# First k and q ahead of the weights, table work reordered, fourteen weight tiles in flight with borrowed buffers spread over them

## Chip, cores, metric

One core of a Trainium2 chip. The metric is device time in microseconds (us) of one execution. Ratios are computed from the mean time of one kernel's runs over the mean of the other's runs of the same rounds, so they are not quite the ratio of the medians that stand beside them.

## The reference, cut to what matters

A linear ("hedgehog") attention over 8 batches, 8 heads, 576 tokens and head size 64 is followed by a spectral mixing layer on the 512 channels:

```python
k_p, q_p = phi(k), phi(q)              # exp of +- (x @ w_phi - max|x @ w_phi|)
kv = einsum('bhsf,bhsd->bhfd', k_p, v);  z = k_p.sum(2)
x = (q_p @ kv) / (q_p . z + 1e-6)      # -> (8, 576, 512)
X = rfft(x, axis=1)[:, :64]            # 64 modes
Yr = Xr @ w_r - Xi @ w_i               # w_r, w_i: 64 x 512 x 512 float32, one matrix per mode
Yi = Xr @ w_i + Xi @ w_r
u = x + irfft(Y, n=576);  out = u + relu(u @ w_ch)
```

The two weight tensors are 67 MB each. They are what most of the run consists of loading.

## The kernel before

Channels are worked in four groups `g` of 128 (two heads each). A group's attention has four units (two batches each), 16 units in all, numbered `n` in a software pipeline. When the four units of group 0 are done, its 16 weight tiles (8 modes of `w_r` or `w_i`, 128 x 8 x 512, cast by the load from float32 to bf16, 1 MB) can be mixed in. Long before that, weights are loaded ahead, into a pool of eight buffers and into "borrowed homes": tensors that are not used yet.

```python
def home(g, w):                      # where weight tile w of group g lives
    if g == 0 and w < 2:             # yacc: two homes
        t = yacc...[:, 4096 * w:4096 * w + 4096]
    elif g == 0 and w == 2:          # the other group's XT buffer
        t = XTb[1]...
    elif g == 0 and w in (10, 11):   # xs of groups 2 and 3
        t = xs[:, w - 8]...
    else:
        return pw.tile([128, MG, DMODEL], BF16, name="wt", tag="wt")   # pool, bufs=8

def next_w(n):                       # issue the next n weight loads, on POOL's DMA queue
    for _ in range(n):
        if wq: key = wq.pop(0); wts[key] = wload(*key)

def some(n):                         # do the next n mixes
        key = mixq.pop(0); mix(*key, wts.pop(key), ...)
        if key == (0, 2): clear(XTb[1])
        if key not in held: next_w(1)        # a freed pool buffer takes the next tile
held = [(0, mg) for mg in (0, 1, 2, 10, 11)] # borrowed homes: nothing handed back
# --- start (cut) ---
units[0].load_k(); next_w(1)         # k0, weight 0, then the identity, then q0, v0
...
units[1].load_k(); units[1].load_v(); next_w(1); units[1].load_q()
for n in range(-2, 17):              # the pipeline over units (cut)
    ...   # group 0's mixes begin at n == 4: some(2), some(1), some(1), some(4)
    if R:  R.turn_k(..); unit(n + 4).load_k()   # k of a later unit into the buffer just turned
           R.turn_q(..); unit(n + 4).load_q()
    if n < 3: next_w((1, 3, 3, 2, 2)[n + 2])    # 2 + 11 = 13 tiles before the first mix
```

Loads of k, q and weights go through one queue, POOL's, in the order of issue; v goes through SP's queue. The traces show an engine keeping to the order of its program: in the kernel before, PE's first row products need only kT, which ACT had copied by 12.2 us, but they stand behind the transposes of q0 and start at 17.29.

## Time and profile before

| kernel before | |
|---|---|
| median (3 runs ahead of the prediction; 4 with the result) | 466.84; 466.88 us |
| span of the profiled run | 467.1 us |
| q0 landed; first row products on PE | 16.02; 17.29 us |
| landing to landing in a full queue: weight tile; k or q tile | 5.05; 1.42 us |
| first weight load that waited for a freed pool buffer, issued | 107.2 us |
| last weight landed; from there to the end | 422.89; 44.2 us |

The landings are read from the trace, DMA by DMA. First the page of the kernel before: the span in 40 slices of 11.7 us, with the DMA engines' busy share in tenths and what they moved.

```profile
DMA  8999999999999999999999999999999999992797
GB/s 193 207 177 220 226 210 228 229 229 136 225 208 229 229 213 222 229 209 227 229 229 207 229 207 208 207 207 207 207 214 214 216 216 211 207 177 50 241 317 254
```

The digit is 9 almost everywhere, so the kernel looks evenly bound by DMA until slice 36. The second row shows what the first hides: the third slice moved 177 and the tenth 136 GB/s, where weights alone run at 207 and v loads lift a slice to 229. The same in windows of 4 us (busy time of each engine with its number of instructions, granted PE clock, DMA share, GB/s):

```profile
core 0: us, PE busy (x) PEld busy (x) DVE busy (x) ACT busy (x) POOL busy (x), PEclk, DMA share, GB/s
28.00:32.00 4.00, 3.35 (x26) 2.58 (x25) 0.69 (x2) 3.22 (x6) 2.01 (x3) 1.00 1.03 159
32.00:36.00 4.00, 2.99 (x23) 1.76 (x24) 3.44 (x5) 3.88 (x6) 2.05 (x3) 1.00 1.07 152
...
104.00:108.00 4.00, 1.75 (x19) 1.16 (x19) 2.59 (x7) 3.20 (x10) 0.78 (x1) 0.93 0.70 117
108.00:112.00 4.00, 4.00 (x54) 3.35 (x52) 1.07 (x4) 1.47 (x4) 0.58 (x2) 0.64 0.92 137
112.00:116.00 4.00, 4.00 (x63) 3.14 (x63) 1.83 (x4) 3.01 (x6) 3.14 (x5) 1.00 1.18 169
```

The share adds up the packets' times, so it passes 1 where packets overlap, and a full queue shows 1.2 and over here; these are the two stretches where it ran dry. The timeline of POOL, which issues, tells why for the second (start, length, what, and in brackets how long POOL sat idle and for whom):

```profile
90.51 0.70 POOL L37 DMA_DIRECT2D kb<-in_k_dram  x1 [12.26 <-PE one L37]
91.63 0.71 POOL L37 DMA_DIRECT2D qb<-in_q_dram  x1 [0.42 <-PE one L37]
107.22 0.89 POOL L37 DMA_DIRECT2D wt<-in_moe_w_i_dram  x1 [14.87 <-PE one L37]
111.53 0.70 POOL L37 DMA_DIRECT2D kb<-in_k_dram  x1 [3.42 <-PE one L37]
```

POOL had nothing it was allowed to issue for nearly 15 us: all homes were full, and the q tile issued at 91.63 was the last in the queue; it landed at 108.23. Last, the start on PE, and PE's last two mixes of a weight tile:

```profile
16.07 1.28 PE L37 MATMUL one<-ident_b,qb 128*128 128x128 bf16 x10 [8.98 <-DMA qb<-in_q_dram]
17.29 1.89 PE L37 MATMUL two<-w2blk,kT 128*128 128x256 bf16 x8
...
417.88 0.67 PE L37 MATMUL pt<-wt,XT 128*32 128x512 bf16 x8 [0.73 <-DMA wt<-in_moe_w_r_dram]
422.94 0.67 PE L37 MATMUL pt<-wt,XT 128*32 128x512 bf16 x8 [1.67 <-DMA wt<-in_moe_w_i_dram]
```

PE waits 8.98 us for q0, and at the end it waits for the last weight tile. After that come 44 us that can't begin earlier.

### The profile page before, as it was taken

To read this page: it belongs to the slowest core of one execution; us is meant where nothing else is said; L and a number is where in the kernel's file an instruction comes from. 1 tells how busy PE (TensorE), PEld (TensorE's weight loads), DVE (VectorE), ACT (ScalarE), POOL (GpSimd) and SP (SyncE) were. 2 spreads that over 40 slices of the span, in tenths; PEclk is the share of its full clock that TensorE was granted. 3 is DMA by queue.
4 is the path that set the end of the run, shared out by engine and by line. 5 is a ranking of instruction groups with operands and counts; after the bars stand their busy time and mean duration, and the time that the engine had idled before them with its cause. 6 is when DMAs were issued, how large, how long until landed. Compare 5 with 4: busy or idle time off the path is not lost.

```text
span 467.1 us, 9757 instructions
## 1 busy us (share of the span) xinstructions
PE 337.8 (72%) x4084; PEld 207.5 (44%) x4084; DVE 269.1 (58%) x488; ACT 281.1 (60%) x475; POOL 92.7 (20%) x130
## 2 busy tenths in 40 slices
PE   0377677758788777788768778129997656997991
PEld 0246465636565555466546546005443322332330
DVE  5275877564666566777675676563331113773882
ACT  2566988766787786688777765123443323664771
POOL 5130322104112121122210112203221110000331
PEclk9998999888888798799997989659998997999996
DMA  8999999999999999999999999999999999992797
GB/s 193 207 177 220 226 210 228 229 229 136 225 208 229 229 213 222 229 209 227 229 229 207 229 207 208 207 207 207 207 214 214 216 216 211 207 177 50 241 317 254
DMA packets 86301, 99.27 MB, mean 213 GB/s; under 512 B 2800, under 2 KB 79728, under 8 KB 86256
## 3 DMA queue, kind: packets, MB, share of 16 engines
q0 software_dynamic: 77264, 81.80, 102.9%
q1 hardware_dynamic: 8992, 16.85, 11.8%
q8 instruction: 32, 0.52, 0.4%
q14 instruction: 13, 0.11, 0.1%
HBM read 163.64 MB, written 9.44 MB: 371 GB/s over the span
## 4 chain that ended last, share of the span: by engine, by line
issue 37%; DMA 21%; PE 16%; ACT 8%; POOL 8%; DVE 7%; POOLq 0%; ACTq 0%
PE pt L37 8%; DMA wt<-in_moe_w_r_dram 8%; DMA wt<-in_moe_w_i_dram 6%; DMA kb<-in_k_dram 5%; PE one L37 4%; POOL wt L37 4%; PE two L37 4%; DVE m L37 4%; ACT AQ L37 3%; DMA qb<-in_q_dram 3%; POOL out_dram L37 2%; ACT AB L37 2%; DVE zall L37 2%; ACT qT L37 1%; ACT kT L37 1%
## 5 line engine op out<-in xcount | busy, mean ns | idle before, releaser
L37 ACT CAST xw<-pt 128x512 bf16<-128x512 f32 x72 | 42.0, 586 | 59.5 <-PE pt L37 58.3
L37 ACT ACTIVATE AB<-two 128x1024 bf16<-128x1024 f32 x64 | 62.8, 1051 | 7.5 <-DVE mk L37 5.1
L37 ACT ACTIVATE AQ<-two 128x1024 bf16<-128x1024 f32 x64 | 63.1, 1055 | 2.8 <-PE two L37 2.6
L37 PE MATMUL pt<-wchb,xT 128*128 128x512 bf16 x144 | 38.6, 393 | 19.3 <-DVE xT L37 19.3
L37 DVE TENSOR_REDUCE m<-two 128x8 f32<-128x1024 f32 x32 | 39.2, 1224 | 19.4 <-PE two L37 19.3
L37 DVE TENSOR_REDUCE mk<-two 128x8 f32<-128x1024 f32 x32 | 38.9, 1219 | 19.5 <-PE two L37 19.0
L37 POOL DMA_DIRECT2D wt<-in_moe_w_i_dram x30 | 26.5, 882 | 110.1 <-PE one L37 63.8
L37 POOL DMA_DIRECT2D wt<-in_moe_w_r_dram x29 | 25.6, 881 | 95.7 <-PE one L37 62.0
L37 DVE TENSOR_TENSOR va<-vn,ee 128x1152 bf16<-128x1152 f32 x32 | 42.0, 1356 | 0.0
L37 DVE RECIPROCAL rd<-one 128x6 f32<-128x6 f32 x48 | 9.4, 196 | 50.3 <-PE one L37 50.3
L37 ACT COPY kT<-one 128x512 bf16<-128x512 bf16 (+1 forms) x32 | 19.2, 640 | 30.0 <-PE one L37 30.0
L37 PEld LDWEIGHTS <-minus 96*128 96x128 bf16 x288 | 27.4, 114 | 20.1 <-issue 14.8
L37 DVE TENSOR_TENSOR xs<-pt,xs 128x512 bf16<-128x512 f32 x36 | 24.3, 691 | 18.9 <-PE pt L37 18.5
L37 PE MATMUL two<-qT,w2blk 128*128 128x512 bf16 x64 | 29.9, 467 | 6.3 <-ACT AQ L37 6.3
L37 PEld LDWEIGHTS <-XT 128*32 128x32 bf16 x512 | 18.0, 179 | 35.9 <-issue 22.9
L37 PE MATMUL two<-w2blk,qT 128*128 128x256 bf16 x128 | 21.2, 292 | 16.5 <-ACT AB L37 11.9
L37 DVE COPY xT<-pt 128x512 bf16<-128x512 bf16 x36 | 15.1, 422 | 27.9 <-PE pt L37 27.9
L37 PEld LDWEIGHTS <-xs 128*128 128x128 bf16 x304 | 24.1, 98 | 14.9 <-issue 7.6
L37 PE MATMUL two<-mT,minus 96*128 96x128 bf16 x256 | 30.3, 252 | 0.0
L37 PE MATMUL pt<-wt,XT 128*32 128x512 bf16 x208 | 18.6, 434 | 13.6 <-DMA wt<-in_moe_w_i_dram 9.9
L37 PEld LDWEIGHTS <-qT 128*128 128x128 bf16 x144 | 14.4, 103 | 31.3 <-issue 28.4
L37 DVE TENSOR_TENSOR xs<-one,rd 128x384 bf16<-128x384 f32 x48 | 26.8, 558 | 1.6
(113 smaller groups left out, 679.3 us busy)
## 6 DMA issues: line engine op xcount, KB each, us to landing
wt<-in_moe_w_i_dram POOLq DMA_DIRECT2D x30, 1024.0 KB, 23.7
wt<-in_moe_w_r_dram POOLq DMA_DIRECT2D x29, 1024.0 KB, 23.9
vn<-in_v_dram SPq DMA_DIRECT2D x16, 576.0 KB, 7.8
kb<-in_k_dram POOLq DMA_DIRECT2D x16, 288.0 KB, 17.6
qb<-in_q_dram POOLq DMA_DIRECT2D x16, 288.0 KB, 17.7
out_dram<-of SPq DMA_DIRECT2D x16, 256.0 KB, 5.8
out_dram<-of POOLq DMA_DIRECT2D x16, 256.0 KB, 5.3
yacc<-in_moe_w_r_dram POOLq DMA_DIRECT2D x1, 1024.0 KB, 12.5
```

What stands on the lines that cost most here:

```text
L37: ins = f(*args, **kwargs)
```

## The change

Its intent: let the first unit begin at once, and never let the weight queue run dry. (1) k0 and q0 lead the queue; weight 0 follows after the iotas and the identity. On DVE the memsets and the sine table come first, the identity and the small copies after it. (2) The second weight tile is one that goes to XT (tile 5) and it is issued after q1; two tiles, not one, follow q2. (3) Fourteen tiles before the first mix, and the six borrowed homes are spread over the tiles (0, 3, 5, 9, 12, 13), so that already the second mix hands back a pool buffer.

```diff
-        if g == 0 and w < 2:
-            t = yacc...[:, 4096 * w:4096 * w + 4096]
-        elif g == 0 and w == 2:
+        if g == 0 and w in (0, 9):
+            h = w // 9
+            t = yacc...[:, 4096 * h:4096 * h + 4096]
+        elif g == 0 and w == 5:
             t = XTb[1]...
-        elif g == 0 and w in (10, 11):
-            t = xs[:, w - 8]...
+        elif g == 0 and w in (3, 12, 13):
+            t = xs[:, max(w - 10, 1)]...
     order = list(wq)
+    wq.remove((0, 5))
+    wq.insert(1, (0, 5))
     units[0].load_k()
-    next_w(1)
-    ident_f = ...; make_identity(nc, ident_f)
-    ident_b, minus, m3s: copies and memsets on DVE
     units[0].load_q()
     units[0].load_v()
     (iotas)
-    w2blk: memset and copies on DVE
+    ident_f = ...; make_identity(nc, ident_f)
+    next_w(1)
+    memsets of w2blk, m3s, CF, XT on DVE
     (sine table on DVE and ACT)
+    ident_b, w2blk, minus: copies on DVE
-                if key == (0, 2):
+                if key == (0, 5):
                     clear(XTb[1])
-    held = [(0, mg) for mg in (0, 1, 2, 10, 11)]
+    held = [(0, mg) for mg in (0, 3, 5, 9, 12, 13)]
     units[1].load_k()
     units[1].load_v()
+    units[1].load_q()
     next_w(1)
-    units[1].load_q()
-            next_w((1, 3, 3, 2, 2)[n + 2])
+            next_w((2, 3, 2, 3, 2)[n + 2])
```

(The views are shortened to "...", and moved lines are told in words.)

More of the change, by code (lines that the diff above doesn't have):

```diff
@@ L316, in home @@
     def home(g, w):
-        if g == 0 and w < 2:
-            t = yacc.bitcast(BF16).rearrange("p o e -> p (o e)")[:, 4096 * w:4096 * w + 4096]
-        elif g == 0 and w == 2:
+        if g == 0 and w in (0, 9):
+            h = w // 9
+            t = yacc.bitcast(BF16).rearrange("p o e -> p (o e)")[:, 4096 * h:4096 * h + 4096]
+        elif g == 0 and w == 5:
             t = XTb[1].rearrange("p s b m -> p (s b m)")[:, 0:4096]
-        elif g == 0 and w in (10, 11):
-            t = xs[:, w - 8].rearrange("p b n d -> p (b n d)")[:, 0:4096]
+        elif g == 0 and w in (3, 12, 13):
+            t = xs[:, max(w - 10, 1)].rearrange("p b n d -> p (b n d)")[:, 0:4096]
         else:
@@ L355 @@
     units[0].load_k()
-    next_w(1)
-    ident_f = scr[:, 2176:2304]
-    make_identity(nc, ident_f)
-    ident_b = const.tile([128, 128], BF16, name="ident_b")
-    dve.tensor_copy(ident_b, ident_f)
-    for t in range(3):
-        r = slice(32 * t, 32 * t + 32)
-        dve.tensor_scalar_mul(out=minus[r], in0=ident_f[r, r], scalar1=-1.0)
-    for m3 in m3s:
-        dve.memset(m3, 0.0)
     units[0].load_q()
@@ L373 @@
     pool.iota(mi, [[4, 2], [8, NO], [1, 4]], base=0, channel_multiplier=0)
-    w2blk = const.tile([128, 256], BF16, name="w2blk")
-    dve.memset(w2blk, 0.0)
-    dve.tensor_copy(w2blk[0:64, 0:128], wpf[0:64, :])
-    dve.tensor_copy(w2blk[64:128, 128:256], wpf[64:128, :])
+    ident_f = scr[:, 2176:2304]
+    make_identity(nc, ident_f)
+    next_w(1)
     def clear(x):
@@ L382, in clear @@
             dve.memset(x[:, i:i + 2], 0.0)
-    clear(XTb[0])
+    w2blk = const.tile([128, 256], BF16, name="w2blk")
     wchb = const.tile([128, 4, 512], BF16, name="wchb")
     CF = const.tile([128, 6, 4, 64], BF16, name="CF")
+    ident_b = const.tile([128, 128], BF16, name="ident_b")
     sf = const.tile([128, 5], F32, name="sf")
+    mf = scr[:, 2112:2176]
+    dve.memset(w2blk, 0.0)
+    for m3 in m3s:
+        dve.memset(m3, 0.0)
+    dve.memset(CF[:, 4:6], 0.0)
+    clear(XTb[0])
     dve.tensor_copy(sf, si)
-    mf = scr[:, 2112:2176]
     dve.tensor_copy(mf, mi)
@@ L410 @@
     act.activation(csf, ang, ACT.Sin, scale=2.0 * math.pi / S_)
+    dve.tensor_copy(ident_b, ident_f)
+    dve.tensor_copy(w2blk[0:64, 0:128], wpf[0:64, :])
+    dve.tensor_copy(w2blk[64:128, 128:256], wpf[64:128, :])
+    for t in range(3):
+        r = slice(32 * t, 32 * t + 32)
+        dve.tensor_scalar_mul(out=minus[r], in0=ident_f[r, r], scalar1=-1.0)
     def forward_table():
-        dve.memset(CF[:, 4:6], 0.0)
         for p0, p1, d, n in ((0, 128, 0, 4), (0, 64, 4, 1), (64, 128, 5, 1)):
```

## The prediction

> What bounds it. The weight stream. In the page's slices the DMA share is 9 nearly everywhere to slice 36. Between landings (issue and landing times of each DMA) a weight tile of 1 MB (bf16) takes 5.05 us, a k or q tile 1.42, and a v load lengthens the gap it falls into by about 1.65. That is 207 GB/s written as bf16, about 414 GB/s read as float32; the Trainium skill, "DMA: Bandwidth & Descriptors", section Bandwidth, measures 425 GB/s for large loads by one core, so the stream has no spare rate. The last weight lands at 422.9 us and its matmuls start at 422.94 after waiting for it; what follows (to 467.1) is a fixed tail of 44 us. So time is won only where the DMA queue runs dry before 422.9.
>
> Where it runs dry (windows of 2 and 3 us, GB/s):
> - 30 to 38 us: 113, 162, 141, 192. The fourth k tile waits until 29.6 us for unit 1's transposes. From landings, about 3.0 us lost.
> - 105 to 120 us: 89, 120, 202, 136, 194. All 13 homes are full; the first mixes (96.4 us) use borrowed homes, which hand no pool buffer back, so the next weight is issued only at 107.2 us. About 4.4 us lost.
> - 0 to 4 us: start, not touched.
>
> What the change does.
> 1. q0 goes ahead of weight 0. Before, q0 landed at 16.02 and PE idled from 7 to 16.07 us. Now q0 should land at 8 to 9. The DVE chain for the sine table now precedes the bf16 identity, so k0's transposes move from 5.9 to about 7 us, which does not matter. The first row products move from 17.3 to about 9.8 us: the attention stage is about 7.4 us earlier throughout, as PE, ACT and DVE pace it (13 to 18 us a unit), and each unit's k and q still land before use.
> 2. Another weight goes ahead of k2, and two follow q2. At about 22 us, when k3 is issued, the queue holds work to about 37 us. The dry stretch at 30 us goes: -3.0 us.
> 3. A fourteenth tile: 5.05 us more work before the first mix. The queue then lasts to about 110 us, and the second mix frees a pool buffer at about 90. The dry stretch at 105 us goes: -4.4 us.
> 4. Moved memsets and copies (2 to 3 us of DVE, 0.3 of POOL): off the path.
>
> On the critical path: items 2 and 3, 7.4 us less a few tenths, as long as compute is as early as the stream, which item 1 gives. I expect 6.6 us: 466.84 -> 460.2 us (-1.4%). Range 458 to 463.5. Chances: faster by over 2% 0.08; within 2% 0.91; slower 0.01.
>
> What would show it: q0 landed before 9 us; first row products near 10; no window between 10 and 400 us under 200 GB/s; last weight landed near 416; last mix still waiting for it; tail near 44 us.
>
> What would make it wrong: PE, not DMA, ending last in the final stage (PE is busy all the time from 394 to 417 us, and waits for the last two tiles only 0.73 and 1.67 us), so that a faster stream is worth less; a later dry stretch because attention did not keep its 7 us; k or q tiles late behind the deeper queue. A gain over 2% would need the tail or the stream's rate to change, which nothing here does.

## The result

| | before | after |
|---|---|---|
| median with the result (4 runs each) | 466.88 us | 461.85 us (460.21 to 462.25) |
| ratio, 95% interval | | 0.9885 (0.9852 to 0.9917) |
| median in a later set of rounds, on chip 6 (11 and 6 runs) | 467.57 us | 461.11 us (460.41 to 461.92) |
| ratio, 95% interval | | 0.9870 (0.9828 to 0.9912) |
| span profiled | 467.1 us | 460.2 us |
| q0 landed; first row products | 16.02; 17.29 us | 10.38; 11.64 us |
| first freed pool buffer reloaded | 107.2 us | 94.6 us |
| last weight landed; from there to the end | 422.89; 44.2 us | 416.38; 43.8 us |

A gain of 1.2 to 1.3%, within 2%. The profiled run of the kernel before took 468.84 us, 2.0 us over its median, and that of after 461.99, about its median; so the profiles show a larger gain (6.9 us in the span) than the first medians (5.0), and about that of the later ones (6.5). The lines of after that answer to those shown of before; first the slices of the page:

```profile
DMA  8999999999999999999999999999999999992897
GB/s 192 207 216 220 230 229 209 228 229 207 229 230 209 228 229 227 209 230 229 207 229 228 207 207 207 206 208 207 207 213 218 214 211 211 205 178 55 249 323 252
```

The digits are nearly the same; in the second row the 177 and the 136 are gone. The windows:

```profile
28.00:32.00 4.00, 3.78 (x79) 3.05 (x79) 3.01 (x3) 3.49 (x5) 0.45 (x1) 1.00 1.24 207
32.00:36.00 4.00, 2.48 (x28) 1.68 (x22) 2.62 (x4) 3.37 (x8) 0.00 (x0) 1.00 1.16 264
...
104.00:108.00 4.00, 4.00 (x43) 3.41 (x42) 1.10 (x3) 1.82 (x4) 0.70 (x1) 0.50 1.23 207
108.00:112.00 4.00, 4.00 (x61) 3.15 (x61) 2.81 (x6) 2.49 (x4) 2.94 (x4) 0.92 1.23 207
112.00:116.00 4.00, 2.88 (x48) 1.84 (x47) 3.43 (x5) 4.00 (x6) 1.14 (x2) 1.00 1.25 207
```

The timeline of POOL around the first freed buffers:

```profile
86.55 0.70 POOL L37 DMA_DIRECT2D kb<-in_k_dram  x1 [10.43 <-PE one L37]
88.31 0.71 POOL L37 DMA_DIRECT2D qb<-in_q_dram  x1 [1.07 <-PE one L37]
94.61 0.87 POOL L37 DMA_DIRECT2D wt<-in_moe_w_r_dram  x1 [5.59 <-PE one L37]
96.21 0.87 POOL L37 DMA_DIRECT2D wt<-in_moe_w_i_dram  x1 [0.73 <-PE one L37]
```

The q tile issued at 88.31 lands only at 110.71, so at 94.61 the queue still held 16 us of work. The start and the end on PE:

```profile
10.42 1.28 PE L37 MATMUL one<-ident_b,qb 128*128 128x128 bf16 x10 [1.62 <-DMA qb<-in_q_dram]
11.64 1.89 PE L37 MATMUL two<-w2blk,kT 128*128 128x256 bf16 x8
...
411.36 0.68 PE L37 MATMUL pt<-wt,XT 128*32 128x512 bf16 x8
416.42 0.67 PE L37 MATMUL pt<-wt,XT 128*32 128x512 bf16 x8 [1.67 <-DMA wt<-in_moe_w_i_dram]
```

The attention stage starts 5.65 us earlier, and the last weight lands 6.5 us earlier and is still waited for. The 44 us behind it did not change.

### The profile page after: what moved, and what is told of

It is laid out like the page before. It is cut to its first block, busy times and chain, and to the rows that moved or that the text cites. A ratio compares the mean times of both kernels' runs of the same rounds, so it can differ in the third digit from the quotient of the medians.

```text
span 460.2 us, 9716 instructions
## 1 busy us (share of the span) xinstructions
PE 331.6 (72%) x4041; PEld 207.1 (45%) x4084; DVE 270.0 (59%) x488; ACT 281.6 (61%) x475; POOL 92.4 (20%) x130
## 4 chain that ended last, share of the span: by engine, by line
issue 27%; PE 23%; ACT 15%; DMA 15%; DVE 13%; POOL 5%; POOLq 0%; ACTq 0%
PE one L37 9%; PE pt L37 8%; DMA wt<-in_moe_w_i_dram 7%; PE two L37 6%; DVE m L37 6%; DMA kb<-in_k_dram 6%; ACT AB L37 5%; ACT AQ L37 5%; DVE mk L37 2%; POOL wt L37 2%; POOL out_dram L37 2%; DMA qb<-in_q_dram 2%; DVE zall L37 2%; ACT kT L37 2%; ACT XT L37 1%
## 5 line engine op out<-in xcount | busy, mean ns | idle before, releaser
L37 PE MATMUL pt<-wchb,xT 128*128 128x512 bf16 x135 | 39.8, 412 | 20.0 <-DVE xT L37 19.7
L37 POOL DMA_DIRECT2D wt<-in_moe_w_i_dram x28 | 24.5, 876 | 91.0 <-PE pt L37 46.1
L37 PEld LDWEIGHTS <-minus 96*128 96x128 bf16 x288 | 26.3, 110 | 19.0 <-issue 13.4
L37 PE MATMUL two<-mT,minus 96*128 96x128 bf16 x256 | 29.3, 245 | 3.1 <-issue 1.9
L37 POOL DMA_DIRECT2D kb<-in_k_dram x16 | 11.5, 716 | 95.5 <-PE one L37 94.7
L37 PE MATMUL one<-kvz,AQ 128*128 128x65 bf16 x512 | 28.0, 211 | 0.0
```

Source lines behind the costliest of these rows:

```text
L37: ins = f(*args, **kwargs)
```

## The experiments

Eleven kernels ran, all with 6 runs against 11 of the kernel before on the same chip; all but the short-stream one compute what the reference asks for (the check passed that one too). One row each; "reload" is the issue of the first weight load into a freed pool buffer, "end" the span less the last landing:

| run | what | first rows | reload | last landing | span | end | median | ratio (95%) |
|---|---|---|---|---|---|---|---|---|
| before | | 17.29 | 107.2 | 422.89 | 467.1 | 44.2 | 466.88 | 1 |
| after | | 11.64 | 94.6 | 416.38 | 460.2 | 43.8 | 461.85 | 0.9885 (0.9852-0.9917) |
| e1_kq_first | start alone | 11.49 | 99.6 | 416.23 | 460.7 | 44.5 | 462.69 | 0.9887 (0.9838-0.9935) |
| e2_deep_only | all but the start | 17.45 | 95.9 | 416.45 | 460.1 | 43.7 | 461.86 | 0.9856 (0.9817-0.9895) |
| e3_twelve | after, 12 tiles | 11.59 | 92.7 | 416.95 | 461.2 | 44.3 | 462.30 | 0.9875 (0.9835-0.9915) |
| e4_ten | after, 10 tiles | 12.18 | 92.9 | 422.79 | 466.3 | 43.5 | 467.31 | 0.9969 (0.9926-1.0012) |
| e5_short | after, 2 tiles less to load | 11.33 | 90.0 | 405.67 | 449.5 | 43.8 | 451.70 | 0.9697 (0.9637-0.9758) |
| e6_v_behind | after, v0 and v1 later | 10.40 | 93.3 | 416.24 | 459.3 | 43.1 | 461.23 | 0.9871 (0.9829-0.9913) |
| e7_old_tables | after, DVE order of before | 12.79 | 93.9 | 415.80 | 460.0 | 44.2 | 461.68 | 0.9885 (0.9843-0.9926) |
| e8_early_only | before, a tile one unit earlier | 16.86 | 108.2 | 423.98 | 468.9 | 44.9 | 467.81 | 0.9994 (0.9949-1.0039) |
| e9_mixed_only | before, homes spread | 16.77 | 95.4 | 418.21 | 461.6 | 43.4 | 463.43 | 0.9911 (0.9870-0.9953) |
| e10_fourteen_only | before, a 14th tile | 16.64 | 114.3 | 421.45 | 465.4 | 44.0 | 467.63 | 0.9987 (0.9944-1.0031) |

The eleventh, after_again, is the changed kernel itself on the chip of e5 to e7:

> The changed kernel again, unchanged, so that the runs of this set have it on the same chip: 460 to 462.5 us, ratio to before about 0.987.

Its span was 459.4 us, its last weight landed at 415.27 us, and it came out at 461.11 us, ratio 0.9870. That landing is 1.1 us before that of the first profile of the same kernel, so single landings are good to about a microsecond.

Each experiment is an edit of the kernel named in the table. The theory throughout: the last weight landing plus 44 us is the time, and the landing moves only with dry stretches of the queue.

### e1_kq_first: the start alone

```diff
 (before, with the start of after: k0 and q0 lead, weight 0 and the identity
  behind the iotas, DVE in the new order; homes, counts and held as before)
```

> Kernel before with only the start of the change: first k and q lead the queue, tables in the new order; homes, queue order and number of weight tiles (13) as before. My prediction on record put the gain on the other two parts (a further weight tile in time, a fourteenth tile) and said that this part alone would move mainly issue times: that theory expects about 466.9 us. The rival, worked out from the landings since: attention starts 5.6 us earlier, so k3 is issued at about 24 us instead of 29.6 while the queue lasts to about 31.5, and the first pool buffer is handed back at about 101.6 us instead of 107.2 while the queue lasts to about 105. Then no dry stretch is left and the time is that of the change, about 461.9 us, last weight landing near 416.5 us.

Measured: 462.69 us, and both stretches gone. (The prediction has no sentence that this part would "move mainly issue times"; it gives this part no microseconds of its own and needs it only so that "compute is as early as the stream".) k3 was issued at 23.87 us and the queue's last weight then landed at 31.51; the first freed buffer was reloaded at 99.55 us, while the queue's last tile landed at 105.71. Its windows:

```profile
28.00:32.00 4.00, 3.78 (x88) 2.95 (x88) 2.21 (x2) 3.49 (x5) 0.07 (x1) 0.67 1.24 207
32.00:36.00 4.00, 1.36 (x16) 0.94 (x14) 3.50 (x7) 3.34 (x9) 0.00 (x0) 1.00 1.15 271
...
104.00:108.00 4.00, 4.00 (x65) 3.07 (x62) 1.51 (x4) 2.29 (x4) 2.27 (x4) 0.79 1.24 208
108.00:112.00 4.00, 3.05 (x35) 2.28 (x32) 3.32 (x4) 3.85 (x5) 2.61 (x3) 1.00 1.22 207
```

So the part that I had credited with nothing by itself has, alone, the whole gain as far as the intervals tell. An earlier start moves issue times, and here that is what counts, because both dry stretches are waits for the attention stage's progress.

### e2_deep_only: everything but the start

```diff
 (after, with the start of before: weight 0 ahead of q0, DVE order of before,
  the second weight ahead of q1)
```

> The change without its start: q0 behind weight 0 and tables in the old order, but the new homes, the new queue order and fourteen tiles. Theory (only the dry stretches of the weight stream count): at 29.6 us the queue holds weights until about 37, and the second mix at about 99 us hands back a pool buffer while the queue lasts to about 110, so no dry stretch: about 461.9 us, last weight landing near 416.5 us, though the first row products come at 17.3 us as before. Rival (the earlier start of the attention stage is what pays): about 466.9 us.

Measured: 461.86 us, with first row products at 17.45 us as in the kernel before; the windows of both stretches show 207 and 208 GB/s. The rival (that the gain needs the earlier attention start) falls. With e1, which has the gain from the start alone, this shows that the two halves of the change replace each other; neither adds anything clear of noise to the other.

### e3_twelve and e4_ten: how deep is deep enough

```diff
 e3_twelve:
-        elif g == 0 and w in (3, 12, 13):
+        elif g == 0 and w == 3:
-    held = [(0, mg) for mg in (0, 3, 5, 9, 12, 13)]
+    held = [(0, mg) for mg in (0, 3, 5, 9)]
-            next_w((2, 3, 2, 3, 2)[n + 2])
+            next_w((2, 3, 2, 2, 1)[n + 2])
 e4_ten: also without the homes for tiles 3 and 5; held (0, 9); next_w((2, 3, 2, 1, 0)[n + 2])
```

> The changed kernel with twelve tiles in flight at first (the two homes in xs for tiles 12 and 13 given up). Theory: the queue then lasts to about 100.6 us and the first pool buffer is handed back at 94.6, an issue takes about 3 us to move data, so still nothing is dry: 461.9 us, as the change. Rival (fourteen in flight is what pays): about 5 us slower per tile beyond the thirteen of before, so about 467 us or more.

> The changed kernel with ten tiles in flight at first (also the homes in XT and in xs for tile 3 given up). Theory: the queue lasts to about 90.5 us and the first pool buffer is handed back at 94.6, with about 3 us from issue to data: about 7 us dry near 91 to 98 us, and time about 7 us over the change, 467 to 470 us; windows there well under 207 GB/s. Rival (the queue's depth does not bound the time): 461.9 us.

Measured: twelve tiles 462.30 us, as the change; ten tiles 467.31 us, its whole gain gone. The windows of the ten-tile kernel:

```profile
84.00:88.00 4.00, 4.00 (x53) 3.31 (x52) 1.72 (x5) 3.51 (x6) 1.40 (x2) 0.70 0.66 95
88.00:92.00 4.00, 1.25 (x18) 0.87 (x20) 3.55 (x4) 3.26 (x4) 0.00 (x0) 1.00 0.59 83
92.00:96.00 4.00, 3.84 (x106) 2.65 (x100) 1.23 (x1) 2.52 (x3) 1.75 (x2) 1.00 0.74 173
```

The stretch is back, some microseconds earlier than I had put it (84 to 96, not 91 to 98 us: the tenth weight had landed at 83.66, and the next k tile was issued only at 84.80), and the last landing is 6.4 us later than in the changed kernel: 422.79 against 416.38. Depth is worth nothing beyond the point where the queue outlasts the wait for the first freed buffer, and below that point it is paid for: two tiles less, 10.1 us of loading, put the last landing off by 5.8 us and the time by 5.0 us (e4 against e3). The 3 us from issue to data in the two expectations fit the kernel before, where a k tile issued at 29.58 into a nearly drained queue landed at 33.74: 4.2 us, of which 1.4 are its own transfer. Of the fourteen tiles, at least two are reserve (eleven was not tried).

### e8_early_only, e9_mixed_only, e10_fourteen_only: the other parts one by one

```diff
 e8_early_only (from before):
-            next_w((1, 3, 3, 2, 2)[n + 2])
+            next_w((2, 3, 2, 2, 2)[n + 2])
 e9_mixed_only (from before): homes {0, 9} in yacc, 5 in XT, {3, 12} in xs
-    held = [(0, mg) for mg in (0, 1, 2, 10, 11)]
+    held = [(0, mg) for mg in (0, 3, 5, 9, 12)]
 e10_fourteen_only (from before): one more home in xs, for tile 3
-    held = [(0, mg) for mg in (0, 1, 2, 10, 11)]
+    held = [(0, mg) for mg in (0, 1, 2, 3, 10, 11)]
-            next_w((1, 3, 3, 2, 2)[n + 2])
+            next_w((1, 3, 3, 2, 3)[n + 2])
```

> Kernel before, where only one of its thirteen tiles is issued a unit earlier (two weights after q2 instead of one, two instead of three two units later). My prediction's sum, in which the two dry stretches are separate terms, expects the first stretch closed and 3 us gained, about 464 us. Rival: with thirteen tiles until the first pool buffer is handed back at 107.2 us, the queue's content up to then is fixed; what isn't lost at 30 us is lost at 105 us, as the queue ends 3 us earlier: last weight landing still near 422.5 us and 466 to 468 us, as before.

Measured: 467.81 us, ratio 0.9994. Its windows (28 to 36 us, then 104 to 112 us):

```profile
28.00:32.00 4.00, 2.10 (x23) 1.72 (x21) 1.84 (x3) 3.64 (x6) 2.84 (x4) 0.89 1.24 206
32.00:36.00 4.00, 3.44 (x47) 2.21 (x48) 2.66 (x3) 3.88 (x5) 1.22 (x2) 0.57 1.25 208
...
104.00:108.00 4.00, 1.74 (x17) 0.97 (x16) 2.76 (x4) 3.19 (x8) 0.00 (x0) 0.92 0.10 29
108.00:112.00 4.00, 3.41 (x32) 2.86 (x33) 1.25 (x6) 1.47 (x6) 0.89 (x1) 0.50 0.62 86
```

The first stretch is closed and the second is deeper: 29 and 86 GB/s where before had 117 and 137. Thirteen tiles are all there is until a buffer comes back at 108 us; loaded without a pause, they are finished earlier and the queue waits the longer (the last tile of the queue landed at 105.74 us, 108.23 in the kernel before). A stretch closed early is given back at the next one that the same buffers end.

> Kernel before, where only the borrowed homes are spread over the tiles (0, 3, 5, 9, 12 instead of 0, 1, 2, 10, 11): thirteen tiles, the same issue counts, the start of before. The first pool buffer comes back with the second mix, at about 98 us instead of 107, while the queue lasts to 108. Theory: the stretch at 105 us closes and that at 30 us stays, so 3.5 to 4.4 us gained, last weight landing near 419 us, 462.5 to 464 us. Rival (the fourteenth tile is what closes it): as before, 466 to 468 us.

Measured: 463.43 us, ratio 0.9911 (0.9870 to 0.9953), with thirteen tiles and nothing else changed. POOL's first two reloads stand at 95.39 and 98.13 us instead of 107.22 and later; the second stretch closes (206 and 208 GB/s from 104 to 112 us) and the first stays (169 and 154 from 28 to 36 us):

```profile
95.39 0.89 POOL L37 DMA_DIRECT2D wt<-in_moe_w_i_dram  x1 [5.49 <-PE one L37]
98.13 0.87 POOL L37 DMA_DIRECT2D wt<-in_moe_w_r_dram  x1 [1.85 <-PE one L37]
```

```profile
28.00:32.00 4.00, 2.64 (x22) 2.01 (x20) 1.29 (x2) 3.73 (x6) 2.52 (x4) 1.00 1.12 169
32.00:36.00 4.00, 2.72 (x42) 1.82 (x43) 3.27 (x4) 4.00 (x5) 1.53 (x2) 0.72 1.10 154
...
104.00:108.00 4.00, 3.17 (x59) 2.76 (x60) 2.19 (x8) 2.78 (x9) 0.70 (x1) 1.00 1.22 206
108.00:112.00 4.00, 4.00 (x62) 3.06 (x60) 3.19 (x7) 3.01 (x6) 3.26 (x4) 1.00 1.24 208
```

This is the one small part, beside the start, that pays on its own.

> Kernel before with a fourteenth tile alone: one more borrowed home (xs, for tile 3), the borrowed homes still first (0, 1, 2, 3, 10, 11), the start of before. The queue then lasts about 5 us longer, to about 113 us, but the first pool buffer comes back only with the fifth mix, at about 113 us instead of 107. Theory: the dry stretch is moved by 6 us and stays about 3 us long, so at most 1.5 us gained: 465 to 467.5 us. My prediction's step (a fourteenth tile closes the stretch): 4.4 us gained, about 462.5 us.

Measured: 467.63 us, ratio 0.9987 (0.9944 to 1.0031). With one more borrowed home in front, four mixes pass before a pool buffer comes back, and the weight load goes from 107.2 to 114.3 us. The timeline of POOL and two windows of this kernel:

```profile
92.19 0.71 POOL L37 DMA_DIRECT2D qb<-in_q_dram  x1 [0.52 <-PE one L37]
112.08 0.71 POOL L37 DMA_DIRECT2D kb<-in_k_dram  x1 [19.17 <-PE one L37]
...
114.32 0.89 POOL L37 DMA_DIRECT2D wt<-in_moe_w_r_dram  x1 [0.52 <-PE one L37]
```

```profile
108.00:112.00 4.00, 3.77 (x45) 3.22 (x46) 0.93 (x3) 1.47 (x6) 0.00 (x0) 0.57 0.92 156
112.00:116.00 4.00, 4.00 (x70) 3.11 (x67) 1.63 (x5) 2.92 (x6) 3.11 (x4) 1.00 0.74 96
```

POOL now sits idle for 19.17 us, and the dry stretch moved from 104-112 to 108-116 us. The title's fourteenth tile is worth nothing clear of noise without the spreading.

### e5_short: is it really the last landing?

```diff
+        n = 4 if g == 1 and w < 4 else MG           # half of four tiles is loaded
-            wt, (moe_w_r, moe_w_i)[i][MG * o:MG * o + MG, ...
+            wt[:, :n], (moe_w_r, moe_w_i)[i][MG * o:MG * o + n, ...
-                    rhs=wt[:, 4 * t + j, :], ...
+                    rhs=wt[:, j if g == 1 and w < 4 else 4 * t + j, :], ...
```

The result is wrong on purpose. A first form, without the last edit, was refused by the check that runs ahead of the chip, since it read parts of a buffer that no load had written, and did not run (it left no page in the record).

> The changed kernel, wrong on purpose: of four weight tiles of group 1 only half is loaded, and its matmuls read the loaded half twice, so PE's work is unchanged and the weight stream is shorter by two tiles, 10.1 us. Theory (the landing of the last weight sets the end, and PE has about 11 us of waits for weights to give in the final stage): 8 to 10 us faster than the change, 452 to 454 us, last weight landing near 406.5 us. Rival of my prediction (PE ends last in the final stage, where it is busy all the time for 25 us): 0 to 3 us faster.

Measured: 451.70 us, 9.4 us under the 461.11 of the same set (8.3 by the means); last landing 405.67, the end 43.8 us. The last mix:

```profile
405.71 0.68 PE L37 MATMUL pt<-wt,XT 128*32 128x512 bf16 x8 [1.12 <-DMA wt<-in_moe_w_i_dram]
```

Even with 10 us less to load PE waits for the last tile in the profiled run (451.29 us). There the rival that my prediction had named, PE ending last in the final stage, falls; three more of the six runs lie within 1.4 us of it. The other two came to 455.62 and 456.55 us, and they have the lowest granted PE clocks (as a share of full speed), 0.891 and 0.882 against 0.906 to 0.920; neither was profiled, so with a stream this short PE may end last in them.

### e6_v_behind and e7_old_tables: the start's own size

```diff
 e6_v_behind (from after):
-            load(self.vn, v, self.g, self.bp, sp)
+            load(self.vn, v, self.g, self.bp, pool if self.g == 0 and self.bp < 2 else sp)
 e7_old_tables (from after): identity, copies and memsets on DVE ahead of the sine table again
```

> The changed kernel with the first two v loads put into the queue of k and q, behind q0 and behind k1, so that they don't share the engines with k0 and q0. Theory: q0 lands near 6.5 us instead of 10.4, the first row products come near 10 us instead of 11.6, as my prediction had it, and the time stays that of the change (within 1 us), as the stream has no dry stretch to close. Rival (each us by which the attention stage starts earlier is worth something): about 1.5 us faster.

Measured: q0 landed at 8.34 us (6.5 expected, a miss of mine; 10.01 in the changed kernel of the same set), first rows at 10.40, time 461.23. That it lands earlier agrees with what the Trainium skill says in "DMA: Bandwidth & Descriptors", section on queues, rings and completion order: each DMA engine takes turns between the queues it has work for. While v0 and v1 run on SP's queue (they landed at 7.74 and 10.80 us in the first profile of after), k0 and q0 get only a part.

> The changed kernel with the DVE work of the start in the order of before (identity, copies and memsets ahead of the sine table). The sine table then ends near 11.5 us and ACT, which works in order, copies kT only after it: first row products near 14.5 us instead of 11.6. Theory: time unchanged (within 1 us), as 14 tiles cover it. Rival: about 3 us slower.

Measured: first rows at 12.79 us, not 14.5, and 461.68 us. The order of the tables sets the start by 1.5 us (12.79 against 11.27 us in the same set) and the time by nothing that the rounds can see.

No tried version beats the changed kernel clearly: e2 and e6 are level with it. The routes left are to load less, as e5 does at the price of the result, or to shorten the 44 us, which nothing here tried.

## Why the prediction was right, point by point

The number was right: 460.2 predicted, range 458 to 463.5, measured 461.85 and later 461.11 us. Not all of the reasoning was.

- **What bounds the kernel: shown.** In thirteen profiles (before, after, and the eleven runs) the span is the last weight landing plus 43.1 to 44.9 us, while the landing ranges over 18 us. e5 moved the landing by 9.6 us (405.67 against 415.27) and the median time by 9.4 us.
- **The stream's full rate: shown.** 5.05 us for a tile that reads 2.1 MB of float32 is 415 GB/s. The skill's 425 GB/s for large loads by one core ("DMA: Bandwidth & Descriptors", Bandwidth) agrees. The change left the rate as it was: 207 GB/s written in both kernels' weight-only windows.
- **The dry stretches and their sum: right within what landings can tell.** 3.0 + 4.4 = 7.4 us predicted; the last landing came 6.5 us earlier in the first profile of after, 7.6 in the second, both against the one profile of the kernel before, whose run was 2.0 us over its median. The medians gained 5.0 and 6.5 us, where 6.6 was predicted.
- **The signs.** No window between 10 and 400 us under 200 GB/s: so it is in the windows of 2 and 3 us up to 162 us, where the stretches had been (the lowest show 204); later, four windows of 2 us show 191 to 199 (at 336, 372, 374 and 394 us), shallow dips beside the 113 and 89 of before. Last landing 416.4 (predicted near 416), last mix still waiting, end 43.8 us: as told. q0 was predicted before 9 us and landed at 10.38, and first rows near 10 us came at 11.64. I had left out that the two v loads share the engines with q0; e6, which takes them away, gets 8.34 and 10.40. The attention stage gained 5.65 us and not 7.4, without consequence.
- **Item 1 as a mere condition ("as long as compute is as early as the stream, which item 1 gives"), with no gain of its own: wrong.** Alone it is worth the whole gain (e1, 0.9887 against the change's 0.9885), because it makes the k tile and the first freed buffer come earlier, and these are what the dry stretches wait for. And as a condition it wasn't needed: e2 has the gain without it.
- **Items 2 and 3 as terms of a sum, -3.0 and -4.4: wrong.** The part of item 2 that closes the first stretch is worth nothing alone (e8, 0.9994): what is saved at 30 us is lost at 105 us, since the number of tiles until the first freed buffer is fixed. The fourteenth tile alone is worth nothing clear of noise (e10, 0.9987). What pays in item 3 is the spreading of the borrowed homes (e9, 0.9911), which frees a pool buffer at the second mix; I had named it, but had credited the stretch to the tile. The sum came out right because the parts together close both stretches whichever way it is divided. That much was luck: the same terms, asked for e8 and e10 alone, gave 464 and 462.5 us, and 467.81 and 467.63 were measured.

Open: the kernel before spreads more than after. Over the three chips of the experiments its runs went from 464.2 to 471.4 us, and the changed kernel's from 460.4 to 461.9 us in its six there. Dry stretches whose length depends on the attention stage could do that, but only one run was profiled, so this stays open. It is not the granted clock in a plain way: the slowest run of all (471.41 us) had 0.904 and the fastest (464.17) 0.901. The spread of e5 (449.9 to 456.6 us) is another matter, as it follows the clock there.

## What to carry to other kernels

When a stream bounds a kernel, look for time in its dry stretches and in its bytes first: here these alone moved the end, and an earlier start with no stretch left to close did not (e6, e7). Find the stretches in GB/s, not in the busy digit. For each stretch compare two times: when the queue ends with what is issued, and when the next buffer comes free; in these runs any part that put the second ahead of the first closed the stretch, further parts were reserve, and a part that only moved one stretch's slack to the next was worth nothing. Put borrowed one-way buffers between recycled ones, not in front of them.

## What the Trainium skill lacked or had wrong

- "DMA: Bandwidth & Descriptors", Anatomy of one DMA, gives 2.0 us plus bytes over 436 GB/s for a load through POOL's queue. An estimate from it for 2.1 MB read is 6.8 us. A weight load that met an almost empty queue took 9.54 us from issue to landing in the kernel before (107.22 to 116.76) and 9.61 in e8 (108.19 to 117.80), and in a full queue the next landing came 5.05 us after the last. In e8 the queue was empty (its last tile had landed at 105.74). The measured loads took 2.7 us more than the estimate; whether the cast is the reason is not shown.
- The same page, Bandwidth: no rate is given for loads that cast. Here a float32 to bf16 load in a full queue took 5.05 us for 2.1 MB read and 1.05 MB written: 415 GB/s by what it reads, near the page's 425, and 207 by what it writes.
- The same page, queues, rings and completion order: it tells that the engines take turns between queues, not what that costs. Here a v load of 590 KB on SP's queue mostly lengthened the POOL queue's landing gap by about 1.65 us, and two of them at the start put q0 off by 1.7 us (10.01 against 8.34 us in e6).
